# Linear attention and a gated FFN: k and q turned by VectorE, projections in 32-row tiles, x by crossbar, one written order

## The chip, the cores and the metric

The kernel runs on one core of a Trainium2 chip, in one launch. The metric is the device time of that launch in microseconds (us), the median of several runs. The core has five engines that matter here: TensorE (PE, matmuls into PSUM), VectorE (DVE), ScalarE (ACT), GpSimd (POOL), and SyncE (SP), which here only issues DMAs. PSUM has eight banks of 128 partitions by 512 fp32 words.

## The reference

Eight batches of eight heads, 576 tokens, head dimension 64; a feature map of 128 features and their negatives; then an FFN over all 4608 tokens.

```python
def phi(x):
    proj = np.einsum('bhsd,df->bhsf', x, w_phi)
    proj = proj - np.max(np.abs(proj), axis=-1, keepdims=True)
    return np.concatenate([np.exp(proj), np.exp(-proj)], axis=-1)
q_p, k_p = phi(q), phi(k)
kv = np.einsum('bhsf,bhsd->bhfd', k_p, v)
z = np.sum(k_p, axis=2)
num = np.einsum('bhsf,bhfd->bhsd', q_p, kv)
den = np.einsum('bhsf,bhf->bhs', q_p, z)[..., None] + 1e-06
attn = num / den                                  # (8, 8, 576, 64)
x = attn.transpose(0, 2, 1, 3).reshape(4608, 512)
out = (np.maximum(x @ w_gate, 0) * (x @ w_val)) @ w_out   # d_ff 1536
```

Since num and den share the factor of a q row, the kernels multiply only the negative half by exp(2 max) and leave the other factor out. The maxima of k enter as exp(-max) and exp(max) that scale v and its column of ones.

## The kernel before

Of each batch's 576 tokens, 512 are worked on as four chunks of 128; the 64 left over of two batches form one mixed chunk. The work comes as steps with a tick each; the steps are sorted by tick and written out in that order, and each engine runs its own instructions in that order. Tiles come from pools (`ps_a` has 5 PSUM banks for the attention, `ps_f` has 3 for the FFN).

- k, two heads at a time (`k_item`): `transposed` turns four blocks of 128x128 with PE (L131), VectorE copies the result out of PSUM (L135). `project_rows` multiplies them by a block diagonal `w2` (L142, 256 columns each) and VectorE reduces 512 projected values of each token row to four maxima (L147). ScalarE takes exp(+p) and exp(-p) (L177). `scale_v` multiplies v by the exponentials of the maxima on GpSimd (L159) and writes the ones column (L165). `k_kv` adds up kv over the chunks with 20 matmuls of 65 columns (L218), and ScalarE copies it out (L223).
- q, two chunks at a time (`q_item_chunks`): the same transposes, eight at a time. q is projected twice: by rows (L142) only for the maxima (L147), and by columns (`q_cols`, L241, 512 columns) with features on partitions for the exponentials (L247). `q_num` multiplies with kv (L263, 65 columns); VectorE scales the negative half into `t` (L279; ScalarE for some of batch 0, L275), adds `u` (L287) and takes the reciprocal (L290); GpSimd normalizes to `xu` (L292). `q_finish` turns `xu` with PE (L299) and VectorE copies it to `xT` (L305).
- FFN, a group of 512 tokens (`ffn_slices`): 12 value and 12 gate steps of four matmuls of 512 columns (L320), each evacuated by ScalarE (L329) or VectorE (L331), then output steps (L342), ScalarE's copy (L352) and the store (L355). There are nine groups, eight batches and the mixed one. The FFN steps of one group lie between the attention steps of the next batch.
- Loads: k and q through GpSimd's queue with a cast to bf16 (L84, L92), v through SP's in fp32, the FFN weights through GpSimd's queue (L116).

Of the kernel before, what the change touches and what calls it, by code (L numbers as in the profile page):

```python
# [14 lines left out]

@with_exitstack
def kernel(
# [11 lines left out]

# [9 lines left out]
    NU = H // 2  # L46
    NFC = DFF // P
    NDC = DM // P
    E = D + 1

    ctx.enter_context(nc.allow_low_precision("bf16 matmuls"))
    ctx.enter_context(nc.allow_non_contiguous_dma("strided loads"))

    singles = ctx.enter_context(tc.tile_pool(name="singles", bufs=1))
    sb_in = ctx.enter_context(tc.tile_pool(name="sb_in", bufs=1))
    sb_mix = ctx.enter_context(tc.tile_pool(name="sb_mix", bufs=1))
    sb_T = ctx.enter_context(tc.tile_pool(name="sb_T", bufs=3))
    sb_f = ctx.enter_context(tc.tile_pool(name="sb_f", bufs=3))
    sb_k = ctx.enter_context(tc.tile_pool(name="sb_k", bufs=5))
    sb_kv = ctx.enter_context(tc.tile_pool(name="sb_kv", bufs=14))  # L60
    sb_s = ctx.enter_context(tc.tile_pool(name="sb_s", bufs=6))
    sb_x = ctx.enter_context(tc.tile_pool(name="sb_x", bufs=2))
    sb_h = ctx.enter_context(tc.tile_pool(name="sb_h", bufs=2))
    sb_g = ctx.enter_context(tc.tile_pool(name="sb_g", bufs=4))
    ps_a = ctx.enter_context(tc.tile_pool(name="ps_a", bufs=5, space=bass.MemoryType.PSUM))
    ps_f = ctx.enter_context(tc.tile_pool(name="ps_f", bufs=3, space=bass.MemoryType.PSUM))

    ctx.enter_context(tc.manual_schedule())

    def psum_a(dtype=FP32):  # L70
        n = 512 if dtype == FP32 else 1024
        return ps_a.tile([P, n], dtype, name="pa", tag="pa")

    def psum_f():
        return ps_f.tile([P, 512], FP32, name="pf", tag="pf")
# [3 lines left out]
    def load_kqv(b, name, src, eng, dtype, heads):  # L79

        t = inputs.get((name, b))
        if t is None:
            t = inputs[name, b] = sb_in.tile([P, H, C, D], dtype, name=f"{name}{b % 2}")
        eng.dma_start(  # L84
            out=t[:, heads],
            in_=src[b, heads, 0:SF, :].rearrange("h (p c) d -> p h c d", c=C),
        )

    def load_mixed(i, name, src, eng, dtype):
        t = inputs[name, i] = sb_mix.tile([P, H, D], dtype, name=name)  # L90
        for bb in range(2):
            eng.dma_start(  # L92
                out=t[SM * bb : SM * (bb + 1)],
                in_=src[2 * i + bb, :, SF:S, :].rearrange("h p d -> p h d"),
            )

    def load_k(b, lo=0, hi=H):
        load_kqv(b, "kn", k, nc.gpsimd, BF16, slice(lo, hi))

    def load_q(b, lo=0, hi=H):  # L100
        load_kqv(b, "qn", q, nc.gpsimd, BF16, slice(lo, hi))

    def load_v(b, lo=0, hi=H, eng=nc.sync):
        load_kqv(b, "vn", v, eng, FP32, slice(lo, hi))

    inputs = {}
    wg_sb = singles.tile([P, NDC, DFF], BF16)
    wv_sb = singles.tile([P, NDC, DFF], BF16)
    wo_sb = singles.tile([P, NFC, DM], BF16)
    xT_mix = singles.tile([P, NDC, SF], BF16)  # L110
    NS = 3
    SPLIT = NFC // 2

    def load_val_gate(t, w, i):
        n = DFF // NS
        nc.gpsimd.dma_start(  # L116
            out=t[:, :, n * i : n * (i + 1)],
            in_=w.rearrange("(c p) n -> p c n", p=P)[:, :, n * i : n * (i + 1)],
        )

    def load_out():
        nc.gpsimd.dma_start(out=wo_sb, in_=moe_w_out.rearrange("(c p) n -> p c n", p=P))
# [3 lines left out]
    def transposed(blocks):  # L126

        n = len(blocks)
        pt = psum_a(BF16)
        for i, blk in enumerate(blocks):  # L130
            nc.tensor.matmul(  # L131
                pt[:, P * i : P * i + P], lhsT=blk, rhs=ident, is_transpose=True
            )
        t = sb_T.tile([P, n, P], BF16, name=f"tT{n}")
        nc.vector.tensor_copy(t.rearrange("p a b -> p (a b)"), pt[:, 0 : n * P])  # L135
        return t

    def project_rows(T2, m):

        pp = psum_a()  # L140
        for i in range(2):
            nc.tensor.matmul(  # L142
                pp[:, 2 * F * i : 2 * F * (i + 1)],
                lhsT=T2[:, i, :],
                rhs=w2.rearrange("p a f -> p (a f)"),
            )
        nc.vector.tensor_reduce(  # L147
            m,
            pp.rearrange("p (c f) -> p c f", f=F),
            axis=AX.X,  # L150
            op=ALU.max,
            apply_absolute_value=True,
        )
        return pp

    def scale_v(engs, dst, src, ek):

        for s, eng in enumerate(engs):
            eng.tensor_tensor(  # L159
                dst[:, :, s, 0:D],  # L160
                src,
                ek[:, :, s : s + 1].to_broadcast([P, 8, D]),
                op=ALU.mult,
            )
        engs[0].tensor_copy(dst[:, :, :, D], ek)  # L165

    def k_start(st, blocks, pool):
        st["T"] = transposed(blocks)
        st["pool"] = pool
        st["kp"] = []  # L170
        st["m"] = sb_s.tile([P, 8], FP32, name="mk")

    def k_rows(st, i):
        pp = project_rows(st["T"][:, 2 * i : 2 * i + 2], st["m"][:, 4 * i : 4 * i + 4])
        kp = st["pool"].tile([P, 2, 4, F], BF16, name=f"kp{i}")
        for s, sign in ((0, 1.0), (1, -1.0)):
            nc.scalar.activation(  # L177
                kp[:, s].rearrange("p c f -> p (c f)"), pp, AF.Exp, scale=sign
            )
        st["kp"].append(kp)  # L180
        if i == 1:
            ek = st["ek"] = sb_s.tile([P, 8, 2], FP32, name="ek")
            for s, sign in ((0, -1.0), (1, 1.0)):
                nc.scalar.activation(ek[:, :, s], st["m"], AF.Exp, scale=sign)

    def k_values(st, b, u, engs):
        vs = st["vs"] = sb_k.tile([P, 8, 2, E], BF16, name="vs")
        vn = inputs["vn", b][:, 2 * u : 2 * u + 2].rearrange("p h c d -> p (h c) d")
        scale_v(engs, vs, vn, st["ek"])

    def k_values_mixed(st, i, bb, engs):

        ekm = sb_s.tile([P, 8, 2], FP32, name="ekm")
        nc.vector.tensor_scalar(
            ekm.rearrange("p a b -> p (a b)"),
            st["ek"].rearrange("p a b -> p (a b)"),
            half[:, bb : bb + 1],
            None,
            op0=ALU.mult,
        )  # L200
        vs = st["vs", bb] = sb_mix.tile([P, 8, 2, E], BF16, name=f"vsm{bb}")
        scale_v(engs, vs, inputs["vm", i], ekm)

    def k_kv(st, b, u, copy):
        mixed = km_state[b // 2]
        pk = psum_a()
        kv_ps = pk[:, 0 : 4 * E].rearrange("p (h s e) -> p h s e", h=2, s=2)
        n = 0
        for hh in range(2):
            h = 2 * u + hh  # L210
            for s in range(2):
                for c in range(C + 1):
                    if c < C:
                        lhsT, rhs = st["kp"][hh][:, s, c, :], st["vs"][:, 4 * hh + c, s, :]
                    else:
                        lhsT = mixed["kp"][h // 4][:, s, h % 4, :]
                        rhs = mixed["vs", b % 2][:, h, s, :]
                    nc.tensor.matmul(  # L218
                        kv_ps[:, hh, s, :], lhsT=lhsT, rhs=rhs, start=(n == 0), stop=(n == 19)
                    )  # L220
                    n += 1
        kv = kvs[b, u] = sb_kv.tile([P, 2, 2, E], BF16, name="kv")
        copy(kv.rearrange("p h s e -> p (h s e)"), pk[:, 0 : 4 * E])  # L223

    def q_start(st, blocks):
        st["T"] = transposed(blocks)
        st["m"] = sb_s.tile([P, 2 * len(blocks)], FP32, name=f"mq{len(blocks)}")

    def q_rows(st, i):
        project_rows(st["T"][:, 2 * i : 2 * i + 2], st["m"][:, 4 * i : 4 * i + 4])  # L230
        if 4 * i + 4 == st["m"].shape[1]:
            st["c"] = sb_s.tile(st["m"].shape, FP32, name="cq")
            nc.scalar.activation(st["c"], st["m"], AF.Exp, scale=2.0)

    def q_cols(st, x, slot, lo, par, first):

        if "qp" not in x:
            x["qp"] = sb_f.tile([P, 2, 2, 4, P], BF16, name="qp", bufs=4)
            x["u"] = sb_f.tile([P, 8, E], FP32, name="u")
        pf = psum_f() if first else psum_a()  # L240
        nc.tensor.matmul(  # L241
# [4 lines left out]
        for s, sign in ((0, 1.0), (1, -1.0)):  # L246
            nc.scalar.activation(  # L247
                x["qp"][:, s, slot].rearrange("p a b -> p (a b)"), pf, AF.Exp, scale=sign
            )

    GROUPS = ((0, 3), (3, 3), (6, 2))

    def q_num(st, x, j, batches, place, col, t_act):


# [352 lines left out]
```

## Time and profile before

| what | us |
|---|---|
| median of 3 runs | 428.93 (428.81 to 429.63) |
| span of the profiled execution, first to last instruction | 426.3 |
| difference of that median and the span, what lies around it | 2.6 |
| PE busy in the span | 398.7 |
| VectorE, ScalarE, GpSimd busy | 284.1, 250.9, 159.6 |
| first FFN matmul starts (L320) | 31.5 |

The page gives no other time of the profiled execution than its span, so its own time is taken as span plus 2.6. Busy times come from instruction records, and an instruction's record may overlap with the next one on the same engine: the distance between two starts is less than a record's length. Lines named L are lines of the kernel file before; steps of the changed kernel are named by their two letters.

### The profile page before, as it was taken

The numbers are of one execution on the slowest core, as the hardware profiler recorded it, in microseconds if no ns is written. First come the engines' busy times: TensorE is split into PE (matmuls) and PEld (weight loads), VectorE is DVE, ScalarE is ACT, GpSimd is POOL, SyncE is SP. The second block draws the span as 40 slices with busy tenths as digits, with TensorE's granted clock in tenths as the row PEclk, the third lists the DMA queues.
The fourth block names the chain that finished last, engine by engine and source line by source line (L and its number), as shares of the span: only waits on it lengthen the run. The fifth ranks groups of instructions, "written<-read, shape, count | busy, mean of one in ns | idle before, by whom it ended". The sixth has DMA issues, their size and how long they took to land.

```text
span 426.3 us, 8695 instructions
## 1 busy us (share of the span) xinstructions
PE 398.7 (94%) x3357; PEld 232.9 (55%) x3416; DVE 284.1 (67%) x641; ACT 250.9 (59%) x575; POOL 159.6 (37%) x204
## 2 busy tenths in 40 slices
PE   3777899989999999999999999999999999999995
PEld 1556665645556556555566556555565554444442
DVE  4888569867687679866876699676856795330420
ACT  3984776566667755687567665766667552322321
POOL 8953861176217501574155211870362021000000
PEclk9999999999999999999999999999999999999999
DMA  8997795245413750167015901374020002002004
GB/s 157 199 265 164 108 181 61 75 122 59 56 51 98 128 61 2 61 156 94 2 59 160 116 3 52 71 139 51 26 76 2 1 14 86 2 0 100 0 2 98
DMA packets 45337, 33.66 MB, mean 79 GB/s; under 512 B 12848, under 2 KB 40112, under 8 KB 45296
## 3 DMA queue, kind: packets, MB, share of 16 engines
q0 software_dynamic: 30480, 16.52, 28.1%
q1 hardware_dynamic: 14816, 16.58, 12.4%
q8 instruction: 27, 0.44, 0.4%
q14 instruction: 14, 0.11, 0.1%
HBM read 37.81 MB, written 9.44 MB: 111 GB/s over the span
## 4 chain that ended last, share of the span: by engine, by line
PE 78%; DVE 10%; ACT 4%; POOL 2%; issue 2%; DMA 2%; POOLq 0%; DVEq 0%; ACTq 0%
PE pf L320 40%; PE pf L342 17%; PE pa L142 6%; PE pa L218 5%; PE pa L263 4%; PE pa L241 3%; PE pa L131 3%; DVE u L287 2%; DVE mk L147 2%; DMA qn_117<-in_q_dram 2%; DVE t L279 2%; PE pa L299 1%; POOL xu L292 1%; ACT qp L247 1%; ACT t L275 1%
## 5 line engine op out<-in xcount | busy, mean ns | idle before, releaser
L320 PE MATMUL pf<-xT,wv_sb 128*128 128x512 bf16 (+1 forms) x386 | 96.9, 366 | 3.8 <-DVE xT L305 2.6
L320 PE MATMUL pf<-xT,wg_sb 128*128 128x512 bf16 (+1 forms) x394 | 97.7, 366 | 2.0 <-ACT val_sb L329 1.4
L292 POOL TENSOR_TENSOR xu<-u,r 128x512 bf16<-128x512 f32 x36 | 37.5, 1042 | 164.1 <-DVE r L290 128.9
L329 ACT CAST val_sb<-pf 128x512 bf16<-128x512 f32 (+1 forms) x114 | 65.3, 573 | 52.7 <-PE pf L320 52.3
L247 ACT ACTIVATE qp<-pa 128x512 bf16<-128x512 f32 x128 | 69.5, 604 | 11.9 <-PE pa L241 11.9
L320 PEld LDWEIGHTS <-wg_sb 128*128 128x128 bf16 x456 | 44.4, 98 | 41.6 <-issue 2.1
L320 PEld LDWEIGHTS <-wv_sb 128*128 128x128 bf16 x456 | 43.3, 98 | 36.5 <-issue 3.9
L147 DVE TENSOR_REDUCE mk<-pa 128x4 f32<-128x512 f32 x72 | 48.4, 682 | 11.3 <-PE pa L142 11.1
L263 PEld LDWEIGHTS <-qp 128*128 128x128 bf16 x640 | 33.9, 98 | 21.5 <-issue 0.9
L287 DVE TENSOR_TENSOR u<-pa,t 128x195 f32<-128x195 f32 (+3 forms) x120 | 40.5, 338 | 6.8 <-ACT t L275 0.5
L279 DVE TENSOR_TENSOR t<-pa,cq 128x195 f32<-128x195 f32 (+3 forms) x114 | 37.6, 330 | 4.6 <-PE pa L263 3.8
L352 ACT COPY out_sb<-pf 128x512 f32<-128x512 f32 x36 | 21.3, 592 | 32.4 <-PE pf L342 29.5
L263 PE MATMUL pa<-kv,qp 128*128 128x65 bf16 x640 | 37.9, 193 | 0.9 <-DVE u L287 0.5
L331 DVE SCALAR_TENSOR_TENSOR h_6277<-pf,val_sb 128x512 bf16<-128x512 f32 x12 | 8.3, 692 | 22.8 <-PE pf L320 22.8
L331 DVE SCALAR_TENSOR_TENSOR h_6056<-pf,val_sb 128x512 bf16<-128x512 f32 x12 | 8.3, 692 | 14.5 <-PE pf L320 14.5
L299 PEld LDWEIGHTS <-xu 128*128 128x128 bf16 x144 | 10.7, 98 | 11.7 <-POOL xu L292 3.8
L223 ACT CAST kv<-pa 128x260 bf16<-128x260 f32 x28 | 10.7, 380 | 10.0 <-PE pa L218 9.9
L299 PE MATMUL pa<-ident,xu 128*128 128x128 bf16 x144 | 14.0, 219 | 2.1 <-POOL xu L292 1.6
L331 DVE SCALAR_TENSOR_TENSOR h_566<-pf,val_sb 128x256 bf16<-128x256 f32 (+1 forms) x18 | 9.1, 506 | 8.8 <-ACT val_sb L329 4.1
L331 DVE SCALAR_TENSOR_TENSOR h_1578<-pf,val_sb 128x512 bf16<-128x512 f32 x12 | 8.3, 691 | 9.6 <-ACT val_sb L329 5.7
L305 DVE COPY xT<-pa 128x512 bf16<-128x512 bf16 x32 | 13.3, 417 | 1.9 <-PE pa L299 1.7
L331 DVE SCALAR_TENSOR_TENSOR h_3132<-pf,val_sb 128x512 bf16<-128x512 f32 x12 | 8.2, 686 | 7.3 <-PE pf L320 3.8
(580 smaller groups left out, 776.1 us busy)
## 6 DMA issues: line engine op xcount, KB each, us to landing
out_dram<-out_sb SPq DMA_DIRECT2D x32, 256.0 KB, 2.3
wv_sb<-in_moe_w_val_dram POOLq DMA_DIRECT2D x3, 512.0 KB, 8.2
wg_sb<-in_moe_w_gate_dram POOLq DMA_DIRECT2D x3, 512.0 KB, 9.7
wo_sb<-in_moe_w_out_dram POOLq DMA_DIRECT2D x1, 1536.0 KB, 13.3
vn_1018<-in_v_dram SPq DMA_DIRECT2D x1, 1024.0 KB, 8.9
vn_335<-in_v_dram POOLq DMA_DIRECT2D x1, 1024.0 KB, 13.5
vn_1793<-in_v_dram SPq DMA_DIRECT2D x1, 1024.0 KB, 7.1
vn_2508<-in_v_dram SPq DMA_DIRECT2D x1, 1024.0 KB, 7.2
```

The source lines that it names most:

```text
L142: nc.tensor.matmul(pp[:, 2 * F * i : 2 * F * (i + 1)], lhsT=T2[:, i, :], rhs=w2.rearrange("p a f -> p (a f)"),)
L147: nc.vector.tensor_reduce(m, pp.rearrange("p (c f) -> p c f", f=F), axis=AX.X, op=ALU.max, apply_absolute_value=True,)
L247: nc.scalar.activation(x["qp"][:, s, slot].rearrange("p a b -> p (a b)"), pf, AF.Exp, scale=sign)
L263: nc.tensor.matmul(pn[:, E * (2 * i + s) : E * (2 * i + s + 1)], lhsT=x["qp"][:, s, slot, blk, :], rhs=kvs[b, h // 2][:, h % 2, s, :],)
L279: nc.vector.tensor_tensor(t, ab[:, :, 1], st["c"][rows, col(lo) : col(lo + n - 1) + 1 : col(1) - col(0)][:, :, None].to_broadcast([np_, n, ...
L287: nc.vector.tensor_tensor(x["u"][rows, lo : lo + n], ab[:, :, 0], t, op=ALU.add)
L292: nc.gpsimd.tensor_tensor(x["xu"], x["u"][:, :, 0:D], r.to_broadcast([P, 8, D]), op=ALU.mult)
L299: nc.tensor.matmul(pt[:, P * i : P * i + P], lhsT=x["xu"][:, 2 * i : 2 * i + 2].rearrange("p a d -> p (a d)"), rhs=ident, is_transpose=True,)
L320: nc.tensor.matmul(ps, lhsT=w[:, dc, P * fi : P * fi + P], rhs=xT[:, dc, lo:hi], start=(dc == 0), stop=(dc == NDC - 1),)
L329: nc.scalar.copy(st["val"], ps)
L331: nc.vector.scalar_tensor_tensor(st["h2"][:, fi, lo:hi], ps, 0.0, st["val"], op0=ALU.max, op1=ALU.mult)
L342: nc.tensor.matmul(st["po"], lhsT=st["h2"][:, fi, P * t : P * t + P], rhs=wo_sb[:, fi, :], start=(fi == 0), stop=(fi == NFC - 1),)
```

## The change

Nearly the whole program is written anew; what it computes is the same.

- The order of all steps of all engines is one string, `ORDER`, of 2031 words such as `qc.4.1:3420`: step, arguments, and after the colon the PSUM banks it uses (eight banks named by hand in place of two pools). Buffers are rings of fixed tiles; k, q and v have one input tile each.
- k and q are no longer turned by PE (but for k of batch 0): VectorE turns blocks of 32x32 fp32 words, each word a pair of bf16 values (`kt`, `ku`, `qt`, `mt`). The projections then contract 32 partitions at a time over pairs, twice (`a` = 0, 1), each partition group into its own bank.
- k is projected in items of 2, 3 and 3 heads: `kr` has 24 matmuls of 128 columns; `ke` and `kx` take 384 elements.
- q is projected once only, by columns (`qc`, batch 0 by `qs`). Its maxima over features, which lie on partitions there, come from a transposing reduce (`qx`), a small PE transpose in fp32 (`qy`), a reduce (`qz`) and a block transpose (`qu`).
- x is turned by a DMA transpose on SP's queue (`xt`) in place of PE and VectorE, but for batch 0 (`xp`, `xc`).
- v is loaded with its column of ones in the tile, in rows of 256 bytes, four DMAs a batch (`lv`); the scaling of v (`vs`, GpSimd) takes the ones column along. The mixed tokens of k go with the item of two heads.
- kv is copied out by VectorE (`kd`); batch 0's x is normalized by VectorE (`ny`). Batch 0's FFN group runs in pieces of 128 tokens for 8 of the 12 column blocks (`pv`, `pg`).

The core of the diff:

```diff
-        t = sb_T.tile([P, n, P], BF16, name=f"tT{n}")
-        nc.vector.tensor_copy(t.rearrange("p a b -> p (a b)"), pt[:, 0 : n * P])
+    def do_qt(bk, b, hq):
+        dst = qT_of(2 * b + hq).rearrange("p h m a -> p (h m a)").bitcast(FP32)
+        src = qn_of(b)[:, 4 * hq : 4 * hq + 4].rearrange("p h c d -> p (h c d)").bitcast(FP32)
+        nc.vector.transpose(
+            dst.rearrange("p (h t c) -> p h c t", h=4, c=C),
+            src.rearrange("p (h c d) -> p h c d", c=C, d=R),
+        )
...
+    def do_kr(bk, b, j):
+        T = kT_of(3 * b + j)
+        for n in range(3):
+            for a in range(2):
+                for i in range(4):
+                    r = slice(R * i, R * (i + 1))
+                    nc.tensor.matmul(
+                        bank[bk[i]][:, F * n : F * (n + 1)],
+                        lhsT=T[r, n, :, a],
+                        rhs=w32[r, a, :],
+                        start=(n == 0 and a == 0),
+                        stop=(n == 2 and a == 1),
+                    )
...
+    def q_cols(T, which, banks, n):
+        for a in range(2):
+            for i, bn in zip(which, banks):
+                r = slice(R * i, R * (i + 1))
+                nc.tensor.matmul(
+                    bank[bn][:, 0:n],
+                    lhsT=w32[r, a, :],
+                    rhs=T[r, :, :, a].rearrange("p h m -> p (h m)"),
+                    start=(a == 0),
+                    stop=(a == 1),
+                )
...
+    def do_qx(bk, b, hq, i):
+        nc.vector.tensor_reduce(
+            maxq[:, :, i, 4 * hq : 4 * hq + 4].rearrange("p t h -> p h t"),
+            bank[bk[0]].rearrange("p (h t u) -> p h t u", h=4, u=R),
+            axis=AX.X,
+            op=ALU.max,
+            apply_absolute_value=True,
+            apply_transpose=True,
+        )
...
+    def do_xt(bk, b, i):
+        nc.sync.dma_start_transpose(out=xT_cols(b, i), in_=xu_of(serial(b, i)))
...
+    for word in ORDER.split():
+        name, _, banks = word.partition(":")
+        name, *args = name.split(".")
+        steps[name]([int(x) for x in banks], *(int(x) for x in args))
```

Some other steps of the changed kernel, by engine: PE `kv` (kv sums), `nu` and `mn` (numerators), `fv`, `fg`, `fo` (FFN value, gate, output); VectorE `nt`, `nv`, `nr` (t, u, reciprocal), `ga` (gate); ScalarE `ke`, `qe`, `me` (exponentials), `va`, `oc` (FFN copies); GpSimd `vs`, `vr` (v scaled), `nx` (normalize), `lk`, `lq` and others (loads); SP `od` (store). The order begins and ends so:

```text
lv.0.0 ms.5 ms.2 lk.0.1 wp wq wc lw.0.0 id k0.1:0 if lm.0.1 wd k1.1:0 ms.6 k2.1:1234 ke.0.1.0.0:1
...
fo.8.1.1:5 ga.8.9:7 ga.8.8:6 fo.8.0.1:1 fo.8.1.2:5 oc.8.1:5 fo.8.0.2:1 fo.8.2.0:3 od.7.1 oc.8.0:1
od.8.1 fo.8.2.1:3 fo.8.2.2:3 oc.8.2:3 fo.8.3.0:2 fo.8.3.1:2 fo.8.3.2:2 od.8.0 od.8.2 oc.8.3:2
od.8.3
```

## The prediction

> **What bounds the kernel now.** I read the page's busy times and slices first, then the busy time by stretch, then the groups by form, and at last the timeline, for the distance from one start to the next.
>
> ```profile
> PE 398.7 (94%) x3357; PEld 232.9 (55%) x3416; DVE 284.1 (67%) x641; ACT 250.9 (59%) x575; POOL 159.6 (37%) x204
> PE   3777899989999999999999999999999999999995
> DVE  4888569867687679866876699676856795330420
> DMA  8997795245413750167015901374020002002004
> ```
>
> ```profile
> 30.00:40.00 10.00, 8.21 (x95) 6.30 (x94) 7.70 (x23) 5.73 (x15) 3.00 (x4) 1.00 1.07 235
> ...
> 200.00:250.00 50.00, 49.53 (x437) 29.21 (x445) 36.54 (x82) 32.32 (x72) 17.26 (x21) 1.00 0.41 78
> ...
> 360.00:426.30 66.30, 61.41 (x281) 27.77 (x284) 16.60 (x24) 18.99 (x33) 0.00 (x0) 0.99 0.13 36
> ```
>
> The second view gives busy time of PE, weight loads, VectorE, ScalarE, GpSimd, then the granted clock and DMA. From 100 to 350 us PE is busy 246.8 of 250 us (98.7%) at full clock while VectorE has a quarter free; the first 40 us are thin on PE, and the end is FFN alone. So PE's work sets the time, plus a start that PE can't fill.
>
> A busy time counts overlaps twice. What an instruction really takes is the distance to the next start:
>
> ```profile
> 202.73 0.35 PE L263 MATMUL pa<-kv,qp 128*128 128x65 bf16 x6
> 202.92 0.38 PE L142 MATMUL pa<-w_119,tT_3454 128*128 128x256 bf16 x2
> 203.14 1.03 PE L320 MATMUL pf<-xT,wv_sb 128*128 128x512 bf16 x4
> 204.00 0.35 PE L263 MATMUL pa<-kv,qp 128*128 128x65 bf16 x6
> ```
>
> ```profile
> 208.85 0.68 DVE L147 TENSOR_REDUCE mq_3456<-pa 128x4 f32<-128x512 f32 x1
> 209.45 0.68 DVE L331 SCALAR_TENSOR_TENSOR h_3132<-pf,val_sb 128x512 bf16<-128x512 f32 x1
> 210.04 0.35 DVE L279 TENSOR_TENSOR t<-pa,cq 128x195 f32<-128x195 f32 x1
> 210.43 0.36 DVE L287 TENSOR_TENSOR u<-pa,t 128x195 f32<-128x195 f32 x1
> 210.71 0.28 DVE L279 TENSOR_TENSOR t<-pa,cq 128x130 f32<-128x130 f32 x1
> ```
>
> So on PE a matmul takes 0.031 us at 65 columns (0.19/6, weight load included), 0.108 at 256, 0.216 at 512 (0.86/4), and likewise 0.055 at 128. On VectorE 512 elements take 0.60 (not 0.68), 195 take 0.28 when nothing waits (0.40 where u waits for its t). ScalarE takes 0.475 for 512, GpSimd 1.00.
>
> PE before, by these: FFN 1296 x 0.216 = 280.0; 432 transposes x 0.055 = 23.8; 288 row projections (L142) x 0.108 = 31.1; 72 column projections (L241) x 0.216 = 15.6; 1280 kv and numerator matmuls x 0.031 = 39.7. Sum 390 of the 426.3 us span, so 36 us are lost, some 25 of them in the first 60 us and 4.6 behind the last matmul.
>
> **The change on PE.** Removed: 398 transposes (21.9; batch 0 keeps 18 for k and 16 for x), all of L142 (31.1) and L241 (15.6): 68.6 us. Added: q columns, 14 steps qc of 8 matmuls of 512 on 32 rows, four row tiles side by side: 14 x 8 x 0.216 / 4 = 6.0; 8 steps qs, one row tile each, 8 x 2 x 0.216 = 3.5; mixed q 0.9; k rows, 21 steps kr of 24 matmuls of 128, 504 x 0.055 / 4 = 6.9; batch 0's k2 2.0; 15 small fp32 transposes at an estimated 0.22 = 3.3. Sum 22.6. Net -46: PE has **344 us** of work.
>
> No row of before shows a row tile, so three unknowns. (a) Side by side or one after another: bounds are the sum above and that with the division by 4 left out, 385.8 us, 41 more. I take side by side, since four steps in a row address four different row groups and four different banks. (b) The hand-over between 128-row and 32-row work: none to, at most, the pipeline's depth, which the 65-column row gives as 0.193 us long less 0.031 apart = 0.16. There are 50 such steps, 100 hand-overs: 0 to 16 us. I take half, 8, as no row is near. (c) kr's weight loads: a load costs at most 0.031 (that same row), 24 of them 0.74 against 0.33 of matmul, so 0 to 9 us over 21 steps; I take 4. These can't go below nothing, because they only add to a stream already counted at its fastest.
>
> The Trainium skill speaks against the change at (a) and (b). TensorE: Matmul & The Clock Gate, Measured speedup vs the span model, gives 3.07 times for four row tiles of 512 columns, not 4; taken for the divided terms it would add some 4 us. TensorEngine Tiling (Array Packing), Key Properties, says that changing the tiling mode drains the engine, which would put (b) near its upper end, 8 us more than I take. No run here shows either yet.
>
> **VectorE.** Removed: PSUM copies of transposes (40 x 0.33, 16 x 0.60) and 32 of 36 copies of x (0.33), 33 us. Maxima: 144 x 0.60 = 86 become kx 96 x 0.467 (384 elements: 0.60 less 128/0.96 ns) = 44.8, qx 64 x 0.60 and mx 16 x 0.34, 88.6 in all, with the transposing reduce priced like the plain one of the nearest row (bounds: that, and twice that since a block must fill before it drains, +44). Added: block transposes 16 x 0.60 + 14 x 0.47 + small ones = 21 (same bounds, +21), small reduces 5, kv copies taken over from ScalarE 9, t's of batch 0. By intervals **256 us**. ScalarE 215 (k exps 192 x 0.37 = 71 in place of 68; kv copies gone), GpSimd 158, nearly unchanged: vs now carries the ones column (28 x 1.5 + 14 x 1.0), the x normalization of batch 0 goes to VectorE, k and q DMA issues stay at 0.7 to 0.9 each. None of these binds over the span; where they sit does.
>
> **By stage.** I add up each engine's work along the written order to three marks.
> - To the first FFN piece (pv.0.0): PE 12.7, VectorE 21.8, GpSimd 25.4. GpSimd sets it: the last vs of batch 0 lies at 23 us of its work, at the 90% it shows over the first 20 us plus a first issue at 1.25 gives 27; then kv, its copy, numerators, t, u, reciprocal, normalize, transposes, copy: 5 to 6 us of latency by the rows. **33 us** (before: first L320 at 31.5).
> - To group 2's first FFN step (fv.2.0): VectorE 102.2, PE 92.6 plus 6 of (b) and (c). VectorE's 80.4 us bind. Two engines within some per cent won't fill as PE alone does; I take 95%: 84.6, so **118 us**.
> - From there: PE 251.7 plus 6 of (b), (c), against VectorE 153.6, ScalarE 128. PE binds, at the 98.7% of before: **261 us**. The end behind it costs 4.6 as before.
> Span 33 + 84.6 + 261 + 4.6 = 383.3; the profiled span was 426.3 beside a median of 428.93, so 2.6 more: **386 us**. With full filling and (b), (c) at nothing it is 33 + 80.4 + 251.7 + 7.2 = 372.
>
> Queues: the 32 crossbar transfers replace 128 PE transposes and 32 copies, and stand on SP's queue between output stores and v loads. An xt that waits for GpSimd's normalize holds the stores and the next v load behind it; a store waiting for its ScalarE copy holds the xt behind it, and FFN of that group waits on PE. I cost this at nothing as numerators of the next steps, kv and output matmuls of the group before lie between; without that cover it is the third rival. v now comes in 256-byte rows, 21,500 more packets for seven batches; the hardware queue took 12.4% of 16 engines for 14816 packets, 0.057 us each, so up to 77 us more of 16 engines' time, where DMA was busy 40% of the span: hidden, but in the first 60 us (8 tenths busy) b = 1 adds 11 us, a risk of some us.
>
> **Rivals.**
> 1. Row tiles run one after another, with a drain (slower side). PE work to fv.2.0 is then 110.5 and the rest 275.3: 33 + 96/0.95 + 275.3/0.987 + 7.2 = 420, and with 0.16 for each of 100 hand-overs 436. It is slower than before from 0.10 us per hand-over on. For: no row shows the concurrency. Against: separate banks and rows. Chance 0.09, half of it slower.
> 2. VectorE binds for longer: block transposes and transposing reduces at half rate. Up to fv.2.0 that is 32 qx, 8 mx and half of the transposes, +32 us, later covered by PE. 386 + 22 for the reduces alone = 408, with all 418. For: it is the fullest engine up to 118 us. Chance 0.14.
> 3. x arrives late: a group's last crossbar transfer is short before its first FFN step. Nearest rows: a 256 KB store lands in 2.3 us, a v load in 7.1 to 8.9; at 7, with 3 us covered, 4 us for 8 groups = 32, 418; at 2.3 nothing. Chance 0.10.
> The forecast (372 to 402) has 0.63, and below 371 us, with an earlier start than I count, 0.04.
>
> **Numbers.** 386 us is the forecast's. 371 to 412 holds the forecast, most of rival 2 and half of rival 3, some 0.8. A measurement can tell about 0.2%, 0.9 us. Slower: half of rival 1 and a little of rivals 2 and 3 together, 0.06; same 0.01; faster 0.93.
>
> **What would show it.** Right: PE work by intervals near 350 us, kr near 0.35 to 0.75 us and qc near 0.45 us a step, VectorE 90% busy or more until about 118 us, PE 98% after, first pv near 33 us. Wrong: qc near 1.7 us (rival 1), qx over 1 us (rival 2), waits of PE's FFN on DMA into xT (rival 3).

## The result and the profile after

The changed kernel takes 407.07 us (median of 4 runs, 405.08 to 409.64) beside 429.06 of the kernel before: a ratio of 0.948 (95% interval 0.944 to 0.952), 22 us less. The forecast was 386, 43 less. The profiled execution took 406.72 us, of which 404.7 are its span.

The stretches of the forecast, read from the starts of the same steps in the trace, in us (the right column is the first experiment, told below):

| stretch | forecast | after | e1_store |
|---|---|---|---|
| start to the first FFN piece (pv.0.0) | 33 | 37.55 | 37.7 |
| to group 2's first FFN step (fv.2.0) | 84.6 | 90.4 | 89.6 |
| to the end of the last matmul | 261 | 257.5 | 257.7 |
| behind the last matmul | 4.6 | 19.25 | 4.9 |
| span | 383.3 | 404.7 | 389.9 |

So of the 21 us missing, 15 lie behind the last matmul. The page of the changed kernel shows it before anything else: the last two slices of PE and DVE are empty, while PE is full to there.

```profile
PE 361.8 (89%) x3517; PEld 191.1 (47%) x3517; DVE 275.9 (68%) x657; ACT 237.1 (59%) x560; POOL 158.5 (39%) x175
PE   0567999989998999999999999999999999999900
DVE  1869999999996897499968978997476223104200
PEclk9999999999999999999999999999999999999975
DMA  8979799778735914279139496041212011020011
q1 hardware_dynamic: 57342, 23.27, 24.3%
```

Busy PE fell by 36.9 us, the time by 22. The granted clock drops in the last two slices only, where PE has nothing to do, so it doesn't explain the end.

By stretch (columns as in the forecast's second view: start and end, length, busy time of PE, weight loads, VectorE, ScalarE, GpSimd, then clock, DMA share, GB/s):

```profile
60.00:100.00 40.00, 37.98 (x496) 20.39 (x495) 38.80 (x97) 35.08 (x91) 28.49 (x29) 1.00 0.83 133
200.00:250.00 50.00, 49.64 (x551) 25.93 (x550) 41.59 (x101) 36.20 (x89) 29.19 (x30) 1.00 0.63 115
385.00:390.00 5.00, 0.42 (x2) 0.00 (x0) 0.00 (x0) 0.00 (x0) 0.00 (x0) 1.00 0.13 51
390.00:395.00 5.00, 0.00 (x0) 0.00 (x0) 0.00 (x0) 0.59 (x1) 0.00 (x0) 0.55 0.13 52
```

From 60 to 100 us VectorE is busy 38.8 of 40 us, as the forecast had it, but PE nearly as much, 38.0; from 200 on PE is full. From 385 on nothing works, one copy of 0.59 us apart, but the DMA engines, at a share of 0.13 and 51 GB/s for some 19 us. The chain of waits names the transfer (start, duration, what; "..." stands for rows of 0.04 us and less), and the waits of ScalarE's copy say the same (us in total, times, longest):

```profile
375.92 4.33 PE bank L880 x20
...
380.27 0.59 ACT ob L889
...
380.89 12.43 DMA out_dram<-ob
...
393.42 0.59 ACT ob L889
```

```profile
ACT ob L889 <- DMA out_dram<-ob: 17.8, 5, 10.0
```

A store of 256 KB took 12.43 us to land, where the forecast's row for such stores in the kernel before was 2.3 us. The last copy (L889) had to wait for the output tile that this store still read, and its own store came behind it. The four stores in question are those of the mixed group. The kernel before wrote each as two stores of 64 rows (40 stores: 32 of 256 KB and 8 of 128 KB); the changed one writes each as one store with the two batches as outermost dimension (36 stores of 256 KB). The stores of 256 KB of the kernel before, then of the changed one (the last number is the median time to landing in us):

```profile
out_dram<-out_sb SPq DMA_DIRECT2D x32, 256.0 KB, 2.3
out_dram<-ob SPq DMA_DIRECT2D x36, 256.0 KB, 3.2
```

### The profile page after: what moved, and what is told of

The parts are those of the page before. It is cut to its first block, busy times and chain, and to the rows that moved or that the text cites. A ratio compares the mean times of both kernels' runs of the same rounds, so it can differ in the third digit from the quotient of the medians.

```text
span 404.7 us, 9013 instructions
## 1 busy us (share of the span) xinstructions
PE 361.8 (89%) x3517; PEld 191.1 (47%) x3517; DVE 275.9 (68%) x657; ACT 237.1 (59%) x560; POOL 158.5 (39%) x175
## 3 DMA queue, kind: packets, MB, share of 16 engines
q1 hardware_dynamic: 57342, 23.27, 24.3%
## 4 chain that ended last, share of the span: by engine, by line
PE 74%; DMA 9%; DVE 8%; issue 3%; POOL 2%; ACT 2%; POOLq 0%; DVEq 0%; ACTq 0%; SPq 0%
PE bank L825 41%; PE bank L880 18%; PE bank L578 5%; PE bank L677 3%; DMA out_dram<-ob 3%; PE bank L614 2%; DMA qn<-in_q_dram 2%; PE bank L463 2%; DMA wv<-in_moe_w_val_dram 2%; DMA kn<-in_k_dram 2%; DVE maxq L637 2%; DVE t L698 1%; ACT kp L510 1%; PE bank L851 1%; DVE u L708 1%
## 5 line engine op out<-in xcount | busy, mean ns | idle before, releaser
L843 DVE SCALAR_TENSOR_TENSOR h<-bank,val 128x512 bf16<-128x512 f32 x100 | 66.5, 681 | 58.7 <-PE bank L825 38.6
L880 PE MATMUL bank<-wo,h 128*128 128x512 bf16 x432 | 101.8, 379 | 0.0
L840 ACT CAST val<-bank 128x512 bf16<-128x512 f32 x100 | 57.5, 593 | 65.7 <-PE bank L825 47.5
L510 ACT ACTIVATE kp<-bank 128x384 bf16<-128x384 f32 x192 | 83.0, 508 | 18.8 <-PE bank L501 10.1
L825 PE MATMUL bank<-xT,wv 128*128 128x512 bf16 x352 | 86.6, 379 | 2.9 <-DVE kT L447 1.8
L825 PE MATMUL bank<-xT,wg 128*128 128x512 bf16 x352 | 86.2, 379 | 0.0
L539 POOL TENSOR_TENSOR vs<-vn,ek 128x780 bf16<-128x780 f32 (+3 forms) x48 | 63.6, 1342 | 41.7 <-ACT ek L527 35.1
L629 ACT ACTIVATE qp<-bank 128x512 bf16<-128x512 f32 x128 | 69.3, 620 | 11.6 <-PE bank L614 7.9
L825 PEld LDWEIGHTS <-wv 128*128 128x128 bf16 x400 | 36.6, 98 | 44.5 <-issue 4.9
L518 DVE TENSOR_REDUCE mk<-bank 128x3 f32<-128x384 f32 x96 | 49.3, 540 | 5.6 <-PE bank L463 3.2
L889 ACT COPY ob<-bank 128x512 f32<-128x512 f32 x36 | 21.1, 595 | 44.8 <-PE bank L880 26.0
L637 DVE TRANSPOSE_TENSOR_REDUCE maxq<-bank 128x16 f32<-128x512 f32 x64 | 42.9, 689 | 3.9 <-PE bank L614 2.2
L557 POOL TENSOR_TENSOR vr<-vm,ek 64x260 bf16<-64x260 f32 x32 | 19.7, 616 | 31.2 <-ACT ek L527 29.4
```

The source lines that it names most:

```text
L510: nc.scalar.activation(kp_of(3 * b + j)[:, i, s].rearrange("p n f -> p (n f)"), bank[bk[0]][:, 0 : 3 * F], AF.Exp, scale=(1.0, -1.0)[s],)
L518: nc.vector.tensor_reduce(mk_of(3 * b + j)[:, :, i], bank[bk[0]][:, 0 : 3 * F].rearrange("p (n f) -> p n f", f=F), axis=AX.X, op=ALU.max, ...
L539: nc.gpsimd.tensor_tensor(vs_of(3 * b + j)[:, s, 0:n].rearrange("p n i e -> p (n i) e")[:, :, 0:e], src[:, lo:hi].rearrange("p h i e -> p ...
L629: nc.scalar.activation(qp_of(4 * b + i)[:, s, 4 * hq : 4 * hq + 4].rearrange("p h m -> p (h m)"), bank[bk[0]], AF.Exp, scale=(1.0, -1.0)[s],)
L637: nc.vector.tensor_reduce(maxq[:, :, i, 4 * hq : 4 * hq + 4].rearrange("p t h -> p h t"), bank[bk[0]].rearrange("p (h t u) -> p h t u", h= ...
L825: nc.tensor.matmul(bank[bk[0]], lhsT=w[:, dc, P * f : P * f + P], rhs=xT(g)[:, dc, :], start=(dc == 0), stop=(dc == NDC - 1),)
```

## Experiments on the end

There were two theories for the 15 us. First: a store whose outermost dimension is 2 runs on two DMA engines only, since 2 of 16 is 0.125 and the share stands at 0.13. Second: the wait for a buffer, that is, four output tiles that share a ring of three.

**e1_store**: the store alone, written as before.

```diff
-            dst = out.rearrange("(b s) n -> b s n", s=S)[2 * t : 2 * t + 2, SF:S, :]
+            for bb in range(2):
+                r0 = S * (2 * t + bb) + SF
+                nc.sync.dma_start(out=out[r0 : r0 + SM, :], in_=ob_of(4 * g + t)[SM * bb : SM * (bb + 1)])
+            return
         nc.sync.dma_start(out=dst, in_=ob_of(4 * g + t))
```

> The stores of the mixed group are split into two DMAs of 64 rows each, as the kernel before had them; nothing else. Theory: the end of the changed kernel is long (19.3 us from the last matmul to the end of the span, where 4.6 was predicted) because one store with the shape 2x64x512 goes out through two of the 16 DMA engines: the DMA share there is 0.13 = 2/16. Split by rows of 64, the end takes 4.6 us again, as in the kernel before: span 385.4 + 4.6 = 390.0, with 2.0 around it 392 us. Rival: the end is long because ScalarE's last copy waits for its buffer (9.96 us on the DMA); the buffers stay three, and the time stays over 400.

Measured: 391.14 us (390.13 to 391.67), ratio 0.9095 (0.9073 to 0.9118). The 128 KB stores land in 2.3 us, and the last 5 us of the span are again a copy and one store. DMA issues of e1_store, then its last two stretches:

```profile
out_dram<-ob SPq DMA_DIRECT2D x8, 128.0 KB, 2.3
xT<-xu SPq DMA_TRANSPOSE x28, 2.5
```

```profile
380.00:385.00 5.00, 4.98 (x24) 2.05 (x21) 0.00 (x0) 1.01 (x2) 0.00 (x0) 1.00 0.62 142
385.00:389.90 4.90, 0.00 (x0) 0.00 (x0) 0.00 (x0) 0.58 (x1) 0.00 (x0) 0.74 0.30 69
```

**e2_ring4**: the stores stay as the change has them, and only the last output copy gets a tile of its own (`u`, no longer used by then), so that it waits for no store.

```diff
+    def ob_at(n):
+        return u_of(0).rearrange("p h e -> p (h e)")[:, 0:DM] if n == 4 * B + 3 else ob_of(n)
```

> The stores of the changed kernel as they are, but the last output copy gets a buffer of its own, so that it needn't wait for an earlier store. Theory (two engines): the four mixed stores move through the same two engines at 6 us each whenever they are issued, 380.9 + 4 x 5.9 = 404.5: no gain, 405 to 408 us. Rival (buffer wait): the last copy starts at 385.5 in place of 393.4 and the end comes 8 us earlier, 399 us.

Measured: 406.34 us in one run, beside 407.07: no gain. In the trace the last copy starts at 385.1 us in place of 393.4, and the span still ends at 404.3. So the copy's wait only passed the time on, and the second theory falls; the stores' own time sets the end, as e1_store and the share of 0.13 say.

The Trainium skill, DMA: Bandwidth & Descriptors, section Rules for kernel authors, has this as a rule: an outermost dimension of fewer than 16 confines a DMA to at most that many engines. The share of 0.13 agrees, and two transfers with 64 rows outermost meet the rule.

## Experiments on PE: are the row tiles really side by side?

The timeline of the changed kernel shows one q projection (`qc`, L614, 8 matmuls of 512 columns on 32 rows) between two FFN steps of four (start, length, instructions):

```profile
173.10 0.63 PE L614 MATMUL bank<-qT,w 32*128 32x512 bf16 x8
173.66 1.04 PE L825 MATMUL bank<-xT,wv 128*128 128x512 bf16 x4
```

From start to start `qc` takes 0.56 us; one after another its 8 matmuls would take 8 x 0.216 = 1.73. So they run 3.1 times as fast. `kr`'s 24 matmuls of 128 take 0.447 us against 24 x 0.055 = 1.32: 3.0 times. The four row tiles of a set start 3 to 4 ns apart, the next set 0.24 us later.

The Trainium skill, TensorE: Matmul & The Clock Gate, section Measured speedup vs the span model, gives 3.07 for four row tiles; this case's 3.1 and 3.0 agree.

**e3_serial**: e1_store with the loops turned around, so that the two matmuls of one row group follow each other and no longer four different row groups.

```diff
-        for a in range(2):
-            for i, bn in zip(which, banks):
+        for i, bn in zip(which, banks):
+            for a in range(2):
```

> e1_store with one change in the order of matmuls inside qc, qs, kr and mc: the two matmuls of one row group follow each other, in place of four row groups side by side; the same matmuls, the same results. Theory: the speed of the row tiles comes from four different row groups in a row (their starts lie 3 to 4 ns apart). Then two on the same group can't overlap, only neighbours can: a qc takes 5 x 0.216 + 0.1 = 1.2 us for 0.56, a kr 3 x 5 x 0.055 + 0.1 = 0.9 for 0.45. 14 qc, 21 kr, 4 mc: 8.6 + 10 + 1.2 = 20 us of PE more, of which 11 lie behind the start of group 2's FFN and are added to the end; before that VectorE binds and some of the 9 hide. 11 to 20 us over e1_store: 403 to 412. Rival: PE overlaps them in any order, and the time is that of e1_store.

Measured: 391.77 us, ratio 0.9124 (0.9085 to 0.9164), the same as e1_store within the intervals. The `qc` of the same place takes 0.58 us from start to start:

```profile
172.60 0.64 PE L614 MATMUL bank<-qT,w 32*128 32x512 bf16 x8
173.18 1.04 PE L825 MATMUL bank<-xT,wv 128*128 128x512 bf16 x4
```

By the medians of all steps `qc` takes 0.572 us in place of 0.564, `kr` 0.457 in place of 0.447. My theory that the order of issue makes the concurrency fell: the matmuls overlap as much in either order, with the first four starts of a step 6 to 7 ns apart in place of 3 to 4. So the forecast's reason ("four steps in a row address four different row groups") isn't what carries it.

## Experiments on x: what was the crossbar worth?

**e4_x_by_pe**: e1_store with x turned by PE into a bank (`xp`, 4 matmuls of 128) and copied by VectorE (`xc`) for all batches, most of them 25 to 50 words behind the normalization, each with a bank that is free there in the written order.

```diff
-xt.2.0
+... xp.2.0:7 ... xc.2.0:7
```

> e1_store with x of all batches turned by PE and copied by VectorE (xp, xc, as batch 0 does it) in place of the crossbar; each pair stands some 25 words behind the place of the crossbar transfer, or just before the group's first FFN step, in a bank that is free there. Theory: the crossbar takes 32 x 0.22 = 7 us off PE and 32 x 0.33 = 10.6 off VectorE, and costs nothing itself; undone, some 27 of the 32 lie where PE binds (+6), 5 where VectorE binds (+1.6), and the in-order waits for GpSimd's normalize add 0 to 10: 7 to 18 us over e1_store, 399 to 410. Rival (x late by the crossbar): PE's waits on the transfers cost more than the turns, and the time falls below e1_store.

Measured: 425.45 us (423.25 to 427.58), ratio 0.9896 (0.9842 to 0.995): 34 us slower than e1_store. By the distances between starts on PE, from pv.0.0 to the last step, its work grew by 7.1 us (32 x 4 matmuls of 0.055), and its waits from 12.8 to 42.4. Of these 16.5 lie ahead of `xp` itself and 10.9 ahead of FFN value steps. So the work explains a fifth.

Not all that this counts as waiting is waiting. The clock line of e4_x_by_pe's page shows dips that the page of e1_store doesn't have:

```profile
PEclk9998999969998999999999999999998999999999
```

The granted clock is 0.975 on average in this execution and 0.997 in e1_store's, so up to 9 us (an estimate: 0.022 of 425.8) of the 36 between the two spans may be matmuls at a lower clock. No run here shows why the clock fell.

**e5_x_extra**: is it that x comes late, or that the step is there at all? e1_store with the crossbar kept, and in addition, 45 words behind each transfer, the same turn by PE and a copy by VectorE into a tile that nobody reads.

```diff
 xt.2.0
+... xp.2.0:2 ... xe.2.0:2
```

> e1_store with the crossbar kept, and besides every crossbar transfer an additional turn of the same x by PE and its copy by VectorE into a tile that nobody reads, some 45 words of the order later, when x has long been there. It prices the turning itself (the work that the crossbar took away), without the waits that x by PE brings in the other experiment. Theory: 32 x 0.22 = 7 us of PE and 32 x 0.33 = 10.6 of VectorE; 27 lie where PE binds (+6), 5 where VectorE binds (+1.6), so +7 to +10 over e1_store, 398 to 401 us; the rest of the 34 us that x by PE cost are then waits of PE on GpSimd and VectorE in order. Rival: the turn itself costs most of the 34 us, since every additional bank in use stalls the others: over 410.

Measured: 428.53 us (427.06 to 432.3), ratio 0.9968 (0.9941 to 0.9995). All of e4_x_by_pe's loss is there though x itself comes by the crossbar and in time: 37 us for 32 steps, 1.17 us each, for 0.22 us of PE and a copy whose record is 0.42 us long. The granted clock is 0.992 here, so it can account for no more than some 2 us of the 37. The groups of e5_x_extra show how it gets lost (busy, mean ns, then the idle time just before them and what ended it):

```profile
L748 PE MATMUL bank<-ident,xu 128*128 128x128 bf16 x144 | 13.5, 218 | 19.7 <-ACT val L846 3.5 <-DVE h L849 3.5 <-DVE maxq L638 3.0
L741 DVE COPY w32f<-bank 128x512 bf16<-128x512 bf16 x32 | 13.4, 418 | 17.9 <-PE bank L748 12.9 <-issue 2.4 <-ACT val L846 1.6
```

PE stands 19.7 us ahead of the extra turns, until ScalarE or VectorE has read the bank that they write; then VectorE stands 12.9 us ahead of the copies, until PE has come. Each engine runs its instructions in the written order, so a wait on one is handed to the other. What the crossbar took away was not 0.55 us of work but two such meeting points for each chunk. This price holds for steps put into an order that was made without them; an order made anew around the turns was not tried, and the kernel before, which turns x by PE as well, has PE 98.7% busy from 100 to 350 us.

**e12_x_gap**: e4_x_by_pe with room between the two: most `xc` stand 7 to 16 words behind their `xp` in place of 1 to 5, and most `xp` some 10 words nearer to the normalization.

```diff
-xp.5.0 (27 words behind nx.5.0)  xc.5.0 (4 words behind xp.5.0)
+xp.5.0 (15 words behind nx.5.0)  xc.5.0 (15 words behind xp.5.0)
```

> e4_x_by_pe with another place for the same steps: PE's turn xp stands up to 12 words behind GpSimd's normalize and VectorE's copy xc up to 14 words behind its xp (11 or more for 19 of the 32, a few next to each other where no bank is free for longer), in place of next to each other. Not one instruction more or less. Theory (the price of x by PE is in the order's waits): VectorE, in order, stood 12.9 us at xc until PE had turned x, and PE stood for banks that VectorE had not read; with room between the two steps VectorE's wait falls below 5 us and the run gets 8 to 15 us shorter than 425: 410 to 417. Rival (the work itself, or the bank that is held, has the price): 422 or more.

Measured: 431.76 us, ratio 1.0074 (1.0041 to 1.0108), slower still. The wait was moved, not removed. Waits of e4_x_by_pe, then of e12_x_gap:

```profile
DVE xT L749 <- PE bank L741: 12.9, 18, 2.7
PE bank L824 <- DVE xT L749: 4.5, 8, 0.9
```

```profile
DVE xT L746 <- PE bank L738: 9.2, 5, 3.7
PE bank L821 <- DVE xT L746: 10.8, 9, 1.8
```

VectorE waits 3.7 us less for the turns, and PE's FFN 6.3 us more for the copies, which now come late. My theory that room between the two would pay fell.

## Experiments on the stretch between 38 and 128 us

The forecast said that VectorE binds here. Four kernels took work off one engine and left the rest.

**e6_q_flat**: e1_store with the block transposes of q read and written flat. The changed kernel writes them with a step of four words; the tokens come out in another order, which FFN's operand and the output rows then follow.

```diff
-        nc.vector.transpose(dst.rearrange("p (h t c) -> p h c t", h=4, c=C), src.rearrange("p (h c d) -> p h c d", c=C, d=R))
+        nc.vector.transpose(dst, src)
...
-                rhs=xT(g)[:, dc, :],
+                rhs=xT(g)[:, dc, :].rearrange("p (i c u) -> p c i u", c=C, u=R),   # g < B
```

> e1_store with q's block transpose writing in the order of its blocks (destination step of one word) in place of a destination step of four words; the tokens of x are then in another order, which the FFN's first matmuls undo in their moving operand, and the rows of the store follow. Theory: the transpose takes 1.09 us for 512 words because of the destination's step, as the flat mixed one takes 0.41 for 256; flat it takes 0.69, 0.4 less for each of 16. VectorE binds up to the start of group 2's FFN, where 7 or 8 of them lie: that start comes 3 us earlier and so does the end: 388. Rival 1: a 32x32 transpose of fp32 takes two cycles a word whatever the step: 1.09 stays, 391. Rival 2: the moving operand in runs of 32 columns slows the FFN's matmuls (0.216 each): over 395.

Measured: 390.84 us, ratio 0.9091 (0.9049 to 0.9134), no difference to e1_store. The step itself does what was expected of it; the group in the changed kernel, then in e6_q_flat:

```profile
L605 DVE STREAM_TRANSPOSE qT<-qn 128x512 f32<-128x512 f32 x16 | 17.3, 1089 | 0.6 <-DMA qn<-in_q_dram 0.6
```

```profile
L605 DVE STREAM_TRANSPOSE qT<-qn 128x512 f32<-128x512 f32 x16 | 11.0, 693 | 1.7 <-DMA qn<-in_q_dram 1.7
```

So the strided write costs 0.40 us of 1.09, and no gain from undoing it shows here: fv.2.0 starts at 127.8 us beside 127.3. But only six of the sixteen transposes lie in the stretch, 2.4 us of 6.4, and the granted clock between 38 and 128 us is 0.98 in this trace and 1.00 in e1_store's, which by itself can cost up to 1.8 us. So this run says little on what binds.

**e8_kv_act**: e1_store with the nine copies of kv of batches 1 to 3 on ScalarE (`kc`) in place of VectorE (`kd`).

```diff
-kd.1.2:6
+kc.1.2:6
```

> e1_store with the copies of kv of batches 1 to 3 (9 of them, 0.34 to 0.47 us) on ScalarE, as in the kernel before, in place of VectorE. Theory: VectorE binds from the first FFN piece to group 2's first FFN step (97% busy there) and ScalarE has 14 us free, so 9 x 0.43 = 3.9 us less for VectorE bring that start 2 to 4 us forward and the end with it: 387 to 389. Rival: PE's own order waits for the copies either way and ScalarE's queue is as full at those places: 391 or more.

Measured: 394.45 us, ratio 0.9182 (0.9136 to 0.9228): 3.3 us slower. Windows of e1_store, then of e8_kv_act:

```profile
38.00:128.00 90.00, 85.68 (x1087) 50.92 (x1099) 87.38 (x212) 75.86 (x187) 53.71 (x58) 1.00 0.80 127
```

```profile
38.00:128.00 90.00, 86.47 (x1073) 50.81 (x1085) 82.47 (x198) 75.84 (x187) 51.00 (x56) 0.98 0.78 124
```

VectorE is busy 4.9 us less in these 90 us, in part because they now hold fewer of the steps; from pv.0.0 to fv.2.0 it is 85.4 us in place of 87.0, since six of the nine copies lie there. Yet this stretch takes 92.9 us in place of 89.6, and fv.2.0 starts 2.8 us later, at 130.1. Up to 1.8 us of that can be the granted clock, 0.98 in these 90 us in place of 1.00; even so, were VectorE's work the bound, the stretch would be shorter than before. The copies now stand among ScalarE's exponentials and wait there for kv's sums (1.7 us in two waits); how the rest comes about was not followed further.

**e13_x_pe_half_kx** and **e14_x_pe_three_dc** do the same in the order of e4_x_by_pe, one for each engine. The first takes k's maxima of batches 1 to 3 over half of the features (7.2 us less for VectorE), the second adds up the FFN-in matmuls of groups 0 and 1 over three of four blocks (6.9 us less for PE).

```diff
-            bank[bk[0]][:, 0 : 3 * F].rearrange("p (n f) -> p n f", f=F),
+            bank[bk[0]][:, 0 : 3 * F].rearrange("p (n f) -> p n f", f=F)[:, :, 0 : F // 2 if 1 <= b <= 3 else F],
```

> e4_x_by_pe, with the maxima of k of batches 1 to 3 taken over 64 of the 128 features (the result is another one): 36 x 0.2 = 7.2 us less work for VectorE, all between the first FFN piece (pv.0.0) and group 2's first FFN step (fv.2.0), a stretch of 103 us there. If VectorE binds in it, as the prediction had it, the run is 5 to 7 us shorter than e4's 425.5: 418 to 420. If PE or the waits in order bind, less than 2: 423 or more.

```diff
-        for dc in range(NDC):
+        last = NDC - 1 if g > 1 else NDC - 2
+        for dc in range(last + 1):
```

> e4_x_by_pe, with the FFN's value and gate sums of groups 0 and 1 over three of the four blocks of x (the result is another one): 32 x 0.216 = 6.9 us less work for PE, in the same stretch. If PE binds in it, 5 to 7 us shorter than e4: 418 to 420. If VectorE binds, less than 2: 423 or more. Should both this and the run with half the k maxima give a good part of their work, the stretch goes by a chain that passes through both engines.

Measured: 424.66 and 423.55 us, ratios 0.9888 (0.9848 to 0.9929) and 0.9871 (0.9856 to 0.9886), beside 0.9896 of e4_x_by_pe. The stretch from pv.0.0 to fv.2.0 went from 103.0 to 101.2 and 100.6 us. Within the stretch VectorE's busy time fell from 89.9 to 84.6 us in the one, PE's from 93.5 to 89.3 in the other. Five us off VectorE bring 1.8, four to seven off PE bring 2.4, and about 1 us of either can be the clock (0.94 in e4_x_by_pe's stretch, 0.95 in the other two). Neither engine binds that order by its work alone; in e4_x_by_pe PE stands idle for 9.5 of the 103 us and VectorE for 13.1. For the order with the crossbar e8_kv_act says that VectorE's work is not the bound. Its PE was not lightened, and in e1_store PE is busy 85.3 of the 89.6 us, so whether PE's work sets that stretch stays open.

## An experiment on the start

In the changed kernel pv.0.0 starts 4.5 us later than forecast. Waits of the changed kernel:

```profile
PE bank L485 <- DMA kn<-in_k_dram: 9.6, 2, 7.5
DVE w L341 <- DMA w64f<-in_w_phi_dram: 1.6, 1, 1.6
```

The first k load brings three heads and is waited for 7.5 us. The second line is w_phi, which is read as a broadcast with outermost dimension 2 (`w64f`) and 4 (`w32f`). Both waits lie ahead of GpSimd's last `vs` of batch 0, though, and that ends at 27.2 us, where the forecast has 27. The 4.5 us are lost behind it: pv.0.0 comes 10.4 us later, where the forecast took 5 to 6. PE is slow there (four matmuls of 65 columns and the start of the next one):

```profile
28.52 0.41 PE L578 MATMUL bank<-vs,kp 128*128 128x65 bf16 x4
28.74 0.25 PE L578 MATMUL bank<-vr,kp 128*128 128x65 bf16 x1
...
32.24 0.29 PE L578 MATMUL bank<-vs,kp 128*128 128x65 bf16 x4
32.37 0.19 PE L578 MATMUL bank<-vr,kp 128*128 128x65 bf16 x1
```

Four take 0.22 us up to 32.1 us and 0.13 from there on, though the clock line of the page shows no dip. 65 of kv's 80 matmuls lie in the slow part, which is some 1.5 us (an estimate: 65 x 0.023). The kernel before did its kv sums of batch 0 at the fast pace, 0.15 us for five, from 22.4 us on; this is the pace that the forecast counted with. Why PE is slow until 32.1 us, and what makes up the other 3 us, no run here shows.

**e7_w_phi**: e1_store with these two loads split into two and four by partition groups, `w64f` issued first and `w32f` later.

```diff
-        nc.sync.dma_start(out=w64f, in_=w_phi[None].to_broadcast([2, D, F]))
+        for i in range(2):
+            nc.sync.dma_start(out=w64f[D * i : D * (i + 1)], in_=w_phi)
```

> e1_store with the loads of w_phi split by partition groups (2 of 64 rows, first on the queue, and 4 of 32 rows, later), in place of one DMA whose outermost step repeats the source 2 or 4 times. Theory: those loads go through 2 and 4 engines and land late (the copy of w64 waits 1.6 us on it and stands before the first copy of turned k on VectorE, and the 32-row one holds VectorE until 7.7 us); split, the first projection starts when k is turned, 1.4 us earlier, and the whole run is 1 to 2 us shorter: 389.5. Rival: the start hangs on the load of q and on GpSimd, and nothing changes: 391.

Measured: 390.2 us (389.96 to 394.6), ratio 0.9103 (0.9051 to 0.9155). In the trace every mark is 1.1 to 1.3 us earlier than in e1_store: pv.0.0 at 36.6, fv.2.0 at 126.1, the end of the last matmul at 383.7. So an earlier load moves pv.0.0 with it. The times can't tell the two kernels apart; the gain is shown in one profile only. e1_store, e6_q_flat and e7_w_phi are all faster than both kernels; a kernel with all three edits was not run.

## Why the prediction was right, and where its sum was wrong

1. **The direction and the main term held.** PE's work set the time, and the change took it down. From fv.2.0 on PE is busy 254.8 us of 257.5 by distances between starts (99%), where 251.7 plus 6 of hand-over at 98.7% was forecast (261). No run put back the turning of k and q by PE or q's second projection, so how the gain divides among the parts of the change is not measured.
2. **The failed step: "The end behind it costs 4.6 as before."** The term measured 19.25. I took it over from the profile of before without pricing the new form of the mixed store, although 36 stores where there had been 40 stand in the change. e1_store undoes that and nothing else, and the term is 4.9 and the time 391.14. No rival named it. So 407 lies inside the range by way of a cause that none of its cases held, which is luck.
3. **Row tiles, (a) to (c).** Side by side, as taken; rival 1 is false. Side by side isn't four times, though. Measured against the divided terms, `qc` is 0.13 us longer and `kr` 0.12. An FFN step of four matmuls ahead of a row-tile step takes 0.958 us in place of 0.863, so some 0.1 more for going in. If every step pays that, it is 0.22 us for each of the 35 steps, some 8 us, and with `qs` perhaps 9 to 10, where 12 were taken for (b) and (c). The drain at a change of tiling mode, which the forecast named from the Trainium skill (TensorEngine Tiling (Array Packing), Key Properties), fits this, and it is small: 0.1 us going in.
4. **VectorE, rival 2.** Its main part is false: the transposing reduce takes 689 ns by its record, the plain one of before 682. Its lesser part came true, but not by the reason that the forecast gave (a block must fill before it drains): the block transposes of q take 1089 ns by their records, 693 when they are written flat (e6_q_flat), so it is the strided write. Groups of the kernel before, then of the changed kernel:

```profile
L147 DVE TENSOR_REDUCE mk<-pa 128x4 f32<-128x512 f32 x72 | 48.4, 682 | 11.3 <-PE pa L142 11.1
L637 DVE TRANSPOSE_TENSOR_REDUCE maxq<-bank 128x16 f32<-128x512 f32 x64 | 42.9, 689 | 3.9 <-PE bank L614 2.2 <-ACT qp L629 0.8 <-PE bank L647 0.6
```

5. **"VectorE's 80.4 us bind."** This step failed as well. The stretch took 90.4 instead of 84.6. That VectorE is 97% busy there is as forecast, but e8_kv_act shows that this is no bound: less work for it didn't make the stretch shorter. Nor do the forecast's own sums say so: PE has 92.6 - 12.7 = 79.9 us there, and with the 6 of (b) and (c) 85.9, more than VectorE's 80.4. 85.9 at the same 95% is 90.4, what was measured; but no run took work off PE in this order, so whether PE's work or the waits between the engines set the stretch stays open, and the 95% was a guess.
6. **Rival 3 is false.** The crossbar transfer lands in 2.5 us, and PE's FFN waits for `xT` once, 0.7 us (in e1_store twice, 2.1 us in all). The forecast costed the crossbar's removal of PE and VectorE work by its work; put back into this order, the turns cost 34 us (e4_x_by_pe), five times PE's 7.
7. **The start** measured 37.55 in place of 33. GpSimd's last `vs` came when the forecast had it, at 27 us, although the forecast looked at GpSimd's work alone and PE waited 7.5 us for the first k load on the way: the agreement is in part luck. The term that was too small is the "5 to 6 us of latency" behind it, which measured 10.4, some 1.5 of it because PE's matmuls took 0.055 us in place of 0.031. w_phi is worth 1.1 us (e7_w_phi); what a smaller first k load would save was not tried.
8. **v in 256-byte rows** cost less than was allowed. The hardware queue took 57342 packets in 24.3% of 16 engines' span, 98 us of their time, against 53 before, so 45 more where the forecast allowed 77. Whether the rows delay the start was not tried.

The sum of the stretches: 383.3 + 4.5 (start) + 5.8 (to fv.2.0) - 3.5 (FFN stretch) + 14.65 (end) = 404.7.

## What to carry to other kernels

For every DMA that a change rewrites, count the engines that its outermost dimension gives it, and price the last one on its own; where everything stands still, read the DMA share (0.13 is two of sixteen). A step that is added to a full order of in-order engines costs its waits and not only its work: 0.2 us of PE and a copy cost 1.17 us each here. A busy share of 97% is no proof of a bound: take work away and see whether the mark moves, and look at the granted clock of both traces before reading the difference.

## What the runs showed of the hardware that I had not expected

- Row tiles of 32 rows overlap whether or not neighbours in the written order share a row group: 0.572 against 0.564 us for eight matmuls of 512 columns.
- A reduce that also transposes blocks costs what a plain one does (689 against 682 ns for 512 values out of PSUM). A block transpose does not keep its speed if its result is written with a step: 693 ns flat, 1089 ns with a step of four words, for 512 fp32 words.
- A store with an outermost dimension of two landed in 12.43 us (256 KB, others of its kind in flight), and two stores of 64 rows in 2.3 us each.
- A moving operand read in pieces of 32 elements with a step (e6_q_flat's FFN) costs PE nothing: four matmuls of 512 columns stay at 0.863 us.
